# Attention with packed keys and a squared-ReLU MLP on one core: a contiguous first softmax, a new order of the work, and elementwise pieces offered to GpSimd

## The chip, the cores and the metric

The kernel runs on one core of a Trainium2 chip. The metric is the device time of one execution in microseconds. The engines are named as in the profile: PE is TensorE (matmuls; PEld its weight loads), DVE is VectorE, ACT is ScalarE, POOL is GpSimd, SP is SyncE, which here only issues the output DMAs.

## The reference

```python
# q, k, v: (8, 8, 576, 64)   p: (8, 8, 32, 64)   w_in: (512, 2048)   w_out: (2048, 512)
def sm_attn(qq, kk, vv):
    s = scale * np.matmul(qq, kk.transpose(0, 1, 3, 2))     # scale = 1/8
    s = s - np.max(s, axis=-1, keepdims=True)
    a = np.exp(s)
    a = a / (np.sum(a, axis=-1, keepdims=True) + 1e-09)
    return np.matmul(a, vv)
p_packed = sm_attn(p, k, v)                 # first softmax: 32 packed rows over 576 keys
out = sm_attn(q, p_packed, p_packed)        # second softmax: 576 rows over 32 packed keys
x = out.transpose(0, 2, 1, 3).reshape(8 * 576, 512)
r = np.maximum(x @ w_in, 0.0)
return (r * r) @ w_out                      # (4608, 512)
```

## The kernel before

All matmuls are in bf16. The DMAs that POOL issues convert q, k, v, p and the weights from float32 while they load. The work goes batch by batch (eight batches of 576 tokens, eight heads in two halves of four, called qd below), and a batch is cut into named steps:

- Loads: one DMA for each half of k and q, two for v (four in batch 0), eight pieces of w_in, eight of w_out. k and q share twelve buffers, v has four.
- Tk, Tq: DVE transposes a half of k or q in 32x32 blocks (lines 459 and 454). X: p, transposed the same way, is copied into a block-diagonal tile pT_bd (line 407). G: the values are regrouped on DVE (line 430).
- S1: first scores, four matmuls a half (line 467), their maximum (473, 474), the exponential (481), written through a strided view e1x of five groups of 128 columns, in two instructions with two sums, then the sum of these, a reciprocal and the normalising multiplication (489 to 491). E: five transposes on PE (496) and the copy out of PSUM (500).
- PV: packed values (509). XT: copies of their result into the block-diagonal pq_bd (523) and into ppT (516).
- M: the packed values times w_in, so that the second attention's product and the first MLP matmul become one (533, copies 538 and 541).
- S2: second scores, sixteen matmuls (553) and four for the remaining 64 rows (560), which the order puts first from batch 1 on; maximum and subtraction on DVE (572, 577), the exponential on ACT (583), sum, reciprocal and multiplication on DVE (589 to 595; together with the exponential called C). N: ten transposes on PE (602, 605) and copies out (610).
- F1: sixteen blocks of four matmuls for each batch (618), ReLU out of PSUM on ACT (630; in batch 0 in halves on ACT and DVE, 632) into one of four r buffers, and its square on DVE (640; in batch 0 also on ACT, 638) into gT, which holds two batches.
- F2: 36 output tiles of 128 tokens, sixteen matmuls each (648), into one of two PSUM banks, copied out (o_sb, line 653) and stored by four DMAs.

PSUM: two pairs of banks for S1, S2 and F1, two banks for the small steps, two for F2.

The order in which instructions stand in each engine's queue isn't written by hand. A planner (class Plan) knows for every piece an engine or a choice of engines with an assumed cost, the steps it depends on and the buffers it takes; it places the pieces one after the other, the one that can begin earliest first, with a small bias for each stream of steps, and the instructions are then emitted by planned start. On the chip each engine works through its queue in this order and waits on semaphores.

Of the kernel before, what the change touches and what calls it, by code (L numbers as in the profile page):

```python
# [3 lines left out]

# [11 lines left out]
P = 128  # L16
# [5 lines left out]
J0 = (0, 5, 10, 14)  # L22
FB = 128
WCH = 512
BDW = 384
# [5 lines left out]
class Piece:  # L31
    __slots__ = ("step", "stage", "k", "alts", "start", "end", "alt", "pred", "late", "order", "only")

    def __init__(self, step, stage, k, alts):
        self.step, self.stage, self.k, self.alts = step, stage, k, alts
        self.late = self.only = None

class Step:
# [4 lines left out]
    def __init__(self, name, segs, deps=(), take=(), give=(), lag=0.0, banks=(), free=()):  # L44
        self.name, self.deps, self.take, self.give, self.lag = name, list(deps), list(take), list(give), lag
        self.banks = list(banks)
        self.free_at = [[t or name for j, t in free if j == i] for i in range(len(segs))]
        self.pieces = [[Piece(self, i, k, p) for k, p in enumerate(st)] for i, st in enumerate(segs)]
        self.give_at = [[(p, t or name) for p, j, t in self.give if j == i] for i in range(len(segs))]

class Plan:
# [3 lines left out]
    def __init__(self, slots, nbanks):  # L56
        self.nslots, self.nbanks = slots, nbanks
        self.unit = {}
        self.streams, self.base = [], {}
        self.fill = 0  # L60

    def stream(self, prio, steps):
        self.streams.append((prio, list(steps)))

    def forward(self):

        busy = {e: ([-1.0], [t]) for e, t in self.base.items()}
        slots = {k: [] for k in self.nslots}
        last = {k: 0.0 for k in self.nslots}
        held, done, out = {}, {}, []  # L70
        banks = [(0.0, ())] * self.nbanks
        unit = {}
        pos = [0] * len(self.streams)
        since = [0.0] * len(self.streams)
        pend = []

        def ready(st, t):
            pred = []
            for d in st.deps:
                x = done.get(d)  # L80
                if x is None:
                    return INF, pred
                t = max(t, x[0] + HOP)
                pred.append(x)
            for p, n in st.take:
                s = slots[p]
                m = len(s) - self.nslots[p]
                for j in range(max(0, m), m + n):
                    x = s[j]
                    if x is None:  # L90
                        return INF, pred
                    t = max(t, x[0] + HOP)
                    pred.append(x)
                t = max(t, last[p])
            if st.banks:
                u = pick(st, t)
                if u is None:
                    return INF, pred
                for j in u:
                    t = max(t, banks[j][0] + HOP)  # L100
                    pred.append(banks[j])
            return t, pred

        def pick(st, t):
            best = None
            for k, u in enumerate(st.banks):
                if any(banks[j] is None for j in u):
                    continue
                x = max(t, max(banks[j][0] + HOP for j in u)) + 0.001 * k
                if best is None or x < best[0]:  # L110
                    best = (x, u)
            return best and best[1]

        def gap(e, us, t):

            s0, s1 = busy.setdefault(e, ([-1.0], [0.0]))
            i = bisect_right(s0, t) - 1
            t = max(t, s1[i])
            while i + 1 < len(s0) and s0[i + 1] < t + us - 1e-9:
                i += 1  # L120
                t = max(t, s1[i])
            return t, i

        def greedy(pc, t):
            if t == INF:
                return t
            b = None
            for e, us, _ in pc.alts:
                s = t if e == "-" else max(t, busy[e][1][-1] if e in busy else 0.0)
                if b is None or s + us < b[0]:  # L130
                    b = (s + us, s)
            return b[1]

        def book(e, t, f):
            s0, s1 = busy[e]
            i = bisect_right(s0, t) - 1
            if t - s1[i] < 1e-9:
                s1[i] = f
                if i + 1 < len(s0) and s0[i + 1] - f < 1e-9:
                    s1[i] = s1[i + 1]  # L140
                    del s0[i + 1], s1[i + 1]
            elif i + 1 < len(s0) and s0[i + 1] - f < 1e-9:
                s0[i + 1] = t
            else:
                s0.insert(i + 1, t)
                s1.insert(i + 1, f)

        while True:
            best = None
            for i, (prio, steps) in enumerate(self.streams):  # L150
                if pos[i] >= len(steps):
                    continue
                pc = steps[pos[i]].pieces[0][0]
                key = pc.late
                if best is not None and key is not None and key >= best[0]:
                    continue
                t, pred = ready(pc.step, since[i])
                if key is None:
                    key = greedy(pc, t) + 0.02 * prio
                if t < INF and (best is None or key < best[0]):  # L160
                    best = (key, pc, t, pred, i)
            for x in pend:
                key = x[0].late
                if key is None:
                    key = greedy(x[0], x[1]) + 0.02 * (x[2] - 0.5)
                if best is None or key < best[0]:
                    best = (key, x[0], x[1], x[3], x)
            if best is None:
                break
            _, pc, t, pred, src = best  # L170
            src_t = t
            b = None
            for i, (e, us, _) in enumerate(pc.alts):
                if (pc.only is None or pc.only == i):
                    s = t if e == "-" else gap(e, us, t)[0]
                    if b is None or s + us < b[0]:
                        b = (s + us, s, i, e)
            f, s, a, e = b
            pc.start, pc.end, pc.alt, pc.pred = s, f, a, pred
            if e != "-":  # L180
                book(e, s, f)
            out.append(pc)
            st = pc.step
            if pc.stage == 0:
                pos[src] += 1
                since[src] = s
                prio = self.streams[src][0]
                if st.banks:
                    u = unit[st.name] = pick(st, src_t)
                    for j in u:  # L190
                        banks[j] = None
                for p, k in st.take:
                    held[p, st.name] = range(len(slots[p]), len(slots[p]) + k)
                    slots[p] += [None] * k
                    last[p] = s
                ends = [pc]
            else:
                pend.remove(src)
                prio = src[2]
                ends = src[4]  # L200
                ends.append(pc)
                done[f"{st.name}/{pc.stage}.{pc.k}"] = (f, ((pc, 0.0),))
                if len(ends) < len(st.pieces[pc.stage]):
                    continue
            fin = max(p.end for p in ends)
            i = pc.stage
            lag = st.lag
            for p, taker in st.give_at[i]:
                x = (fin + lag, tuple((q, lag) for q in ends))
                for j in held.pop((p, taker)):  # L210
                    slots[p][j] = x
            for taker in st.free_at[i]:
                for j in unit[taker]:
                    banks[j] = (fin + lag, tuple((q, lag) for q in ends))
            if i + 1 < len(st.pieces):
                hop = 0.0 if e == "-" else HOP
                pr = [(fin + hop - HOP, tuple((q, hop - HOP) for q in ends))]
                state = []
                for q in st.pieces[i + 1]:
                    pend.append((q, fin + hop, prio, pr, state))  # L220
            else:
                done[st.name] = (fin + lag, tuple((q, lag) for q in ends))
        assert all(pos[i] == len(s) for i, (_, s) in enumerate(self.streams)) and not pend, [
            s[pos[i]].name for i, (_, s) in enumerate(self.streams) if pos[i] < len(s)]
        self.made = unit
        return out, max(p.end for p in out)

    def backward(self, out, T):
        late = {}
        busy = {}  # L230
# [687 lines left out]
```

## Time and profile before

| what | value |
|---|---|
| median of the runs | 312.61 us (312.1 to 314.21, three runs) |
| profiled execution | 313.22 us, span 311.5 us from the first to the last instruction |
| PE busy | 249.4 us (80%), 1888 matmuls |
| DVE busy | 203.7 us (65%), 437 instructions |
| ACT busy | 183.1 us (59%), 336 instructions |
| POOL busy | 44.4 us (14%), 76 instructions, nearly all issues of DMAs |
| mean granted PE clock | 0.99 |
| loads from HBM, stores | 37.2 MB, 9.4 MB |

Busy is time in which an engine executes; matmuls overlap in PE's pipeline, so a busy PE isn't one at its peak. The share of busy time is a mean over a start in which PE has little to do and a long stretch in which it has nearly always something; a stretch has to be read for itself.

### The profile page before, as it was taken

The numbers are of one execution on the slowest core, as the hardware profiler recorded it, in microseconds if no ns is written. First come the engines' busy times: TensorE is split into PE (matmuls) and PEld (weight loads), VectorE is DVE, ScalarE is ACT, GpSimd is POOL, SyncE is SP. The second block draws the span as 40 slices with busy tenths as digits, with TensorE's granted clock in tenths as the row PEclk, the third lists the DMA queues.
The fourth block names the chain that finished last, engine by engine and source line by source line (L and its number), as shares of the span: only waits on it lengthen the run. The fifth ranks groups of instructions, "written<-read, shape, count | busy, mean of one in ns | idle before, by whom it ended". The sixth has DMA issues, their size and how long they took to land.

```text
span 311.5 us, 5119 instructions
## 1 busy us (share of the span) xinstructions
PE 249.4 (80%) x1888; PEld 139.8 (45%) x1888; DVE 203.7 (65%) x437; ACT 183.1 (59%) x336; POOL 44.4 (14%) x76
## 2 busy tenths in 40 slices
PE   0243596799759888999899889988999799998883
PEld 0141254355526454655455444545454536653331
DVE  6658588879586957777778775786878575540000
ACT  1433287774877566757785767755885577751110
POOL 7655554304000300021000000000000000000000
PEclk9999999999997999999999999999999999999998
DMA  7999999997900691129411102020202111112222
GB/s 120 199 205 206 206 198 207 208 176 137 222 8 0 109 204 43 47 19 209 103 34 36 51 22 58 11 64 3 69 2 67 36 36 34 34 36 64 53 51 67
DMA packets 26456, 28.44 MB, mean 91 GB/s; under 512 B 5440, under 2 KB 17728, under 8 KB 26432
## 3 DMA queue, kind: packets, MB, share of 16 engines
q0 software_dynamic: 18992, 18.55, 37.6%
q1 hardware_dynamic: 6912, 9.45, 11.3%
q8 instruction: 14, 0.23, 0.3%
q10 hardware_dynamic: 528, 0.13, 0.2%
q14 instruction: 10, 0.08, 0.1%
HBM read 37.22 MB, written 9.44 MB: 150 GB/s over the span
## 4 chain that ended last, share of the span: by engine, by line
PE 59%; DVE 20%; ACT 11%; DMA 4%; issue 4%; POOL 1%; SPq 0%; ACTq 0%; DVEq 0%; POOLq 0%
PE ps L648 33%; PE ps L618 14%; ACT o_sb L387 5%; PE ps L553 2%; PE ps L467 2%; DMA v_b<-in_v_dram 2%; PE ps L532 2%; DVE pq_bd L389 2%; PE ps L602 2%; DMA out_dram<-o_sb 2%; DVE t L589 2%; DVE gT L640 2%; ACT pq_bd L387 2%; DVE n L595 1%; PE ps L509 1%
## 5 line engine op out<-in xcount | busy, mean ns | idle before, releaser
L648 PE MATMUL ps<-w_out_b,gT 128*128 128x512 bf16 x576 | 146.8, 380 | 15.9 <-ACT o_sb L387 14.2
L630 ACT ACTIVATE r<-ps 128x576 bf16<-128x576 f32 (+1 forms) x131 | 76.6, 617 | 19.5 <-PE ps L618 16.2
L648 PEld LDWEIGHTS <-gT 128*128 128x128 bf16 x576 | 54.4, 98 | 68.0 <-issue 17.1
L618 PE MATMUL ps<-a,M 128*128 128x288 bf16 x512 | 80.1, 292 | 5.9 <-ACT M L387 2.0
L618 PEld LDWEIGHTS <-M 128*128 128x128 bf16 x512 | 49.5, 99 | 33.6 <-issue 11.2
L640 DVE TENSOR_TENSOR gT<-r 128x576 bf16<-128x576 bf16 x119 | 51.9, 454 | 16.1 <-ACT r L630 15.0
L387 ACT COPY o_sb<-ps 128x512 f32<-128x512 f32 x32 | 18.8, 587 | 33.2 <-PE ps L648 33.2
L387 ACT CAST M<-ps 128x1024 bf16<-128x1024 f32 (+1 forms) x32 | 29.3, 958 | 14.2 <-PE ps L532 13.6
L481 ACT ACTIVATE e1x<-ps,n 128x320 bf16<-128x320 f32 (+1 forms) x32 | 25.3, 904 | 17.9 <-DVE n L474 17.9
L459 DVE STREAM_TRANSPOSE kT<-k_b 128x1152 bf16<-128x1152 bf16 x16 | 21.3, 1358 | 1.1 <-DMA k_b<-in_k_dram 1.1
L454 DVE STREAM_TRANSPOSE qT<-q_b 128x1152 bf16<-128x1152 bf16 x16 | 21.7, 1364 | 0.0
L467 PE MATMUL ps<-kT,pT_bd 128*128 128x288 bf16 x64 | 11.8, 313 | 11.3 <-DVE kT L459 11.1
L419 POOL DMA_DIRECT2D k_b<-in_k_dram x16 | 8.9, 554 | 72.5 <-DVE kT L459 66.1
L387 ACT COPY e<-ps 128x640 bf16<-128x640 bf16 x15 | 10.4, 692 | 12.3 <-PE ps L509 6.3
L389 DVE CAST pq_bd<-ps 32x64 bf16<-32x64 f32 x32 | 7.0, 219 | 14.7 <-ACT r L630 9.8
L532 PE MATMUL ps<-w_in_b,ppT 64*32 64x512 bf16 x256 | 11.5, 409 | 5.6 <-DVE M L389 2.9
L589 DVE TENSOR_REDUCE t<-e 128x36 f32<-128x1152 bf16 (+2 forms) x10 | 11.1, 1110 | 7.2 <-ACT e L583 7.2
L473 DVE TENSOR_REDUCE m<-ps 128x1 f32<-128x576 f32 x16 | 11.9, 742 | 4.6 <-PE ps L467 4.5
L467 PEld LDWEIGHTS <-pT_bd 128*128 128x128 bf16 x64 | 6.7, 104 | 16.5 <-issue 7.4
L572 DVE TENSOR_REDUCE m<-ps 128x4 f32<-128x128 f32 (+2 forms) x17 | 12.2, 719 | 2.1 <-PE ps L553 1.1
L427 POOL DMA_DIRECT2D v_b<-in_v_dram x18 | 12.2, 684 | 5.0 <-DMA k_b<-in_k_dram 1.8
L583 ACT ACTIVATE e<-d 128x1152 bf16<-128x1152 f32 (+2 forms) x10 | 9.7, 972 | 5.0 <-DVE d L577 4.9
(54 smaller groups left out, 197.9 us busy)
## 6 DMA issues: line engine op xcount, KB each, us to landing
out_dram<-o_sb SPq DMA_DIRECT2D x144, 64.0 KB, 1.7
k_b<-in_k_dram POOLq DMA_DIRECT2D x16, 288.0 KB, 8.4
q_b<-in_q_dram POOLq DMA_DIRECT2D x16, 288.0 KB, 10.3
v_b<-in_v_dram POOLq DMA_DIRECT2D x7, 320.0 KB, 10.3
w_in_b<-in_moe_w_in_dram POOLq DMA_DIRECT2D x8, 256.0 KB, 9.4
w_out_b<-in_moe_w_out_dram POOLq DMA_DIRECT2D x8, 256.0 KB, 10.3
v_b<-in_v_dram POOLq DMA_DIRECT2D x7, 256.0 KB, 10.6
v_b<-in_v_dram POOLq DMA_DIRECT2D x2, 160.0 KB, 6.6
```

Source lines behind the costliest of these rows:

```text
L387: nc.scalar.copy(dst, src)
L389: eng.tensor_copy(dst, src)
L454: nc.vector.transpose(self.qT[:, qd].rearrange("p dh (j a) -> p j dh a", a=32), self.t.q[qd][:].rearrange("p (j dh dl) -> p j dh dl", dh=2 ...
L459: nc.vector.transpose(kT[:, qd].rearrange("p dh (j a) -> p j dh a", a=32), self.t.k[qd][:].rearrange("p (j dh dl) -> p j dh dl", dh=2, dl=32))
L467: nc.tensor.matmul(ps[:, c], lhsT=pT_bd[self.b % 2][:, blk(qd, dh)], rhs=kT[:, qd, dh, c * HALF:(c + 1) * HALF], start=(dh == 0), stop=(dh ...
L481: nc.scalar.activation(e[:, i, :, :n], self.ps1[qd][:, :, x0 * 32:(x0 + n) * 32].rearrange("p c (x a) -> p c x a", a=32), ACT.Exp, bias=se ...
L532: nc.tensor.matmul(pair(u, j)[o:o + 32, qd, :], lhsT=self.ppT[64 * e:64 * e + 64, qd, pr, :], rhs=w_in_b[64 * e:64 * e + 64, qd * 2 + pr, ...
L589: nc.vector.tensor_reduce(self.t2[:, g0:g1], self.e2[:, g0:g1], axis=AX.X, op=ALU.add)
L618: nc.tensor.matmul(ps[:, c], lhsT=a.M[:, qd, fb * FB:(fb + 1) * FB], rhs=a.a2[:, qd, c * HALF:(c + 1) * HALF], start=(qd == 0), stop=(qd = ...
L630: nc.scalar.activation(dst, src, ACT.Relu)
L640: eng.tensor_tensor(out=Att.cols(gT[:, fb, o:o + S]), in0=r, in1=r, op=ALU.mult)
L648: nc.tensor.matmul(po[t], lhsT=gT[:, fb, n0:n0 + P], rhs=w_out_b[:, fb, :], start=(fb == 0), stop=(fb == NFB - 1))
```

## The change

Five things change together.

- First softmax. k is loaded in two DMAs per half, so that the keys lie in an order in which the first scores, taken by six matmuls a half (four of 256 columns, two of 64), come out with their 576 columns in the order of the values. The exponential is one contiguous instruction of 576 columns with one sum. The factor 1/8 is put into p when it is expanded, and with it goes the multiplication of the maximum. p is expanded for batches 0 and 1 and for 2 to 7 together, into a tile that holds all batches, instead of batch by batch.
- Smaller copies. ppT is taken in two copies rather than four; M starts from ppT alone, and the sixteen matmuls of the second scores stand ahead of the four.
- Planner. It becomes a list scheduler: at each moment the ready piece with the best priority starts on the engine that ends it first. A table holds a priority for each step and batch and a bias against ACT. The assumed costs are new.
- Choices of engine. Added: ReLU on DVE in batch 1, M's copies on DVE.
- GpSimd (name Q) is offered the squares of F1, the multiplication of the second softmax, the regrouping of the values and the second expansion of p, where POOLED holds the batch (all of them). It also sets zeros (setup2).

The built program of the changed kernel has on POOL 30 squares (in batches 0 to 6: 3, 5, 3, 7, 4, 6 and 2), one multiplication of 128x128 and the memsets; the regrouping and the expansion of p stay on other engines. Its queue of 576 matmuls of F2 is spread otherwise: between the first F1 blocks of successive batches stand 16, 104, 35, 85, 44, 119 and 71 of them (before: 26, 51, 76, 68, 76, 68, 76), 24 within the last batch's blocks (25) and 78 after them (110).

```diff
+TABLE = {'o': {'F1.6': -46.7, 'Tq.4': -34.44, 'E.6': -81.52, 'E.7': 45.46, 'PV.3': -5.85, 'F1.7': -39.65, 'I2':
...
         def setup():
-            nc.vector.memset(pT_bd[0][:, :BDW + 2 * P], 0.0)
-            nc.vector.memset(e1x[:, :, GM * P:], 0.0)
...
+            nc.vector.memset(pT_bd[:, :2], 0.0)
+            nc.vector.memset(v_b[0][:64, :, GM * D:], 0.0)
...
+        def setup2():
+            nc.gpsimd.memset(pT_bd[:, 2:], 0.0)
+            for i in range(1, NV):
+                nc.gpsimd.memset(v_b[i][:64, :, GM * D:], 0.0)
...
+        def expand_p(b0, b1, h, eng):
...
+                eng.tensor_scalar_mul(dst, src, 0.125)
...
+                    src = k[self.b, qd * QH:(qd + 1) * QH].rearrange("h (j2 a x) d -> j2 h a (x d)", j2=2, x=VX)
+                    for j2 in range(2):
+                        nc.gpsimd.dma_start(t[:, j2 * VX * D:(j2 + 1) * VX * D], src[j2])
...
             def s1(self, qd, u):
-                ps = self.ps1[qd] = pair(u)[:, :, :HALF]
-                for c in range(2):
+                ps = self.ps1[qd] = pair(u).rearrange("p c n -> p (c n)")[:, :S]
+                kv = [kT[:, qd, dh].rearrange("p (j2 x a) -> p x j2 a", j2=2, a=32) for dh in range(2)]
+                w = [pT_bd[:, self.b, qd, dh] for dh in range(2)]
+                main = ps[:, :GM * P].rearrange("p (g i n) -> p i g n", i=2, n=64)
+                for i in range(2):
                     for dh in range(2):
-                        nc.tensor.matmul(ps[:, c], lhsT=pT_bd[self.b % 2][:, blk(qd, dh)],
-                                         rhs=kT[:, qd, dh, c * HALF:(c + 1) * HALF], start=(dh == 0), stop=(dh == 1))
+                        nc.tensor.matmul(main[:, i], lhsT=w[dh], rhs=kv[dh][:, i * GM:(i + 1) * GM],
+                                         start=(dh == 0), stop=(dh == 1))
+                for dh in range(2):
+                    nc.tensor.matmul(ps[:, GM * P:], lhsT=w[dh], rhs=kv[dh][:, 2 * GM], start=(dh == 0), stop=(dh == 1))
...
-                e = e1x[:, qd].rearrange("p (g a i2 i) -> p i i2 g a", i=2, i2=2, a=32)
-                for i, n in (0, GM + 1), (1, GM):
-                    x0 = i * (GM + 1)
-                    nc.scalar.activation(e[:, i, :, :n], self.ps1[qd][:, :, x0 * 32:(x0 + n) * 32].rearrange(
-                        "p c (x a) -> p c x a", a=32), ACT.Exp,
-                        bias=self.n1[:, qd:qd + 1], scale=0.125, accum_out=self.d1[:, qd, i:i + 1])
+                nc.scalar.activation(e1x[:, qd], self.ps1[qd], ACT.Exp, bias=self.n1[:, qd:qd + 1],
+                                     accum_out=self.d1[:, qd:qd + 1])
...
+            return [Step(f"G.{b}.0", [[[("DVE", 0.83, lambda: L[b].group(0, H, V))] + ([("POOL", 3.0, lambda: L[b].group(0, H, Q))] if b in POOLED else [])]],
...
-                        [[("DVE", 0.07 + w / 960, lambda: T[b].s2_mul(x, V))]]]
+                        [[("DVE", 0.08 + w / 900, lambda: T[b].s2_mul(x, V))]
+                         + ([("POOL", 0.4 + w / 700, lambda: T[b].s2_mul(x, Q))] if b in POOLED else [])]]
...
-                res = [Step(nr, [r] + front(2, 128), pre, banks=AB, free=[(2, None)]),
-                       Step(nm, [a] + front(3, 1024), pre, banks=HB, free=[(2, None)]),
+                res = [Step(nm, [a] + front(3, 1024), pre, banks=HB, free=[(2, None)]),
+                       Step(nr, [r] + front(2, 128), pre, banks=AB, free=[(2, None)]),
...
+                sq = [("DVE", 0.46, lambda fb=fb: f1_sq(T[b], fb, V))]
+                if b in SPLIT:
+                    sq.append(("ACT", 0.68, lambda fb=fb: f1_sq(T[b], fb, A)))
+                if b in POOLED:
+                    sq.append(("POOL", 0.95, lambda fb=fb: f1_sq(T[b], fb, Q)))
...
+        POOLED = range(B)
...
+                                          + ([("POOL", 1.0, lambda h=h: expand_p(2, B, h, Q))] if POOLED else []) for h in range(QH)]], ["P.2", "I2"])])
...
+        ld += load_wo(range(0, 4)) + [Step("I2", [[[("POOL", 5.0, setup2)]]])]
...
+        plan.use(TABLE)
+        est = plan.run()
```

## The prediction

> **What bounds the kernel now.** I read the page's table of slices first (where PE is thin), then busy time in ten stretches cut at the first F1 matmul (L618) of each of the eight batches, then the waits of PE, then groups by form. Columns of the first view: from:to, length, busy time and (instructions) of each engine, granted PE clock, DMA share, GB/s.
>
> ```profile
> 0.00:37.60 37.60, 11.23 (x101) 6.79 (x102) 23.79 (x59) 12.14 (x24) 22.60 (x40) 1.00 1.14 187
> 37.60:66.80 29.20, 23.31 (x190) 12.91 (x190) 24.43 (x48) 21.94 (x49) 11.12 (x19) 1.00 1.27 204
> 66.80:99.10 32.30, 27.00 (x218) 15.81 (x217) 25.00 (x54) 22.13 (x40) 3.54 (x6) 0.95 0.54 103
> 99.10:132.90 33.80, 30.54 (x242) 17.35 (x240) 24.52 (x53) 22.34 (x41) 3.55 (x6) 1.00 0.50 93
> 132.90:164.20 31.30, 28.87 (x233) 16.45 (x232) 24.07 (x52) 22.25 (x39) 3.54 (x6) 1.00 0.50 91
> ...
> 276.90:311.50 34.60, 25.34 (x115) 10.98 (x113) 0.90 (x2) 4.75 (x8) 0.00 (x0) 0.96 0.24 61
> ```
>
> Up to 66.8 us PE is not the bound: the loads run at 187 to 204 GB/s and DVE is busy 24 of 37.6 and 24 of 29.2 us. From 99 us on PE is (30.5 of 33.8 us). The next view is who PE waited for after 66.8 us: total us, times, longest.
>
> ```profile
> PE ps L648 <- ACT o_sb L387: 14.2, 23, 0.7
> PE ps L560 <- DVE ppT L389: 6.2, 6, 1.6
> PE ps L618 <- ACT M L387: 2.0, 1, 2.0
> PE ps L618 <- ACT e1x L481: 0.8, 1, 0.8
> PE ps L648 <- DVE gT L640: 0.5, 1, 0.5
> PE ps L532 <- DVE d L577: 0.4, 1, 0.4
> ```
>
> A second output tile starts only after the copy of the one before it, 0.6 us each time (14.2/23): the largest item. Then the four matmuls of the rest of the second scores (L560), which stand ahead of the main sixteen (L553), wait about 1 us in six batches for the ppT copies. The rest falls into the third stretch, and there the clock shows it too:
>
> ```profile
> 84.00:90.00 6.00, 3.87 (x54) 1.95 (x52) 4.95 (x14) 3.92 (x8) 0.00 (x0) 1.00 0.24 79
> 90.00:96.00 6.00, 3.59 (x34) 2.10 (x26) 4.39 (x6) 4.67 (x6) 0.00 (x0) 0.82 0.01 3
> 96.00:99.00 3.00, 3.00 (x21) 1.92 (x21) 1.36 (x4) 1.99 (x4) 0.00 (x0) 0.79 0.00 0
> ```
>
> PE stood idle 4.5 of 12 us between 84 and 96, and the granted clock of 0.82 and 0.79 follows. Prices for the engines that the change moves work between:
>
> ```profile
> L640 DVE TENSOR_TENSOR gT<-r 128x576 bf16<-128x576 bf16 x119 | 51.9, 454 | 16.1 <-ACT r L630 15.0
> L481 ACT ACTIVATE e1x<-ps,n 128x320 bf16<-128x320 f32 x16 | 15.7, 979 | 17.9 <-DVE n L474 17.9
> L481 ACT ACTIVATE e1x<-ps,n 128x256 bf16<-128x256 f32 x16 | 13.3, 829 | 0.0
> L481 ACT ACTIVATION_READ_ACCUMULATOR e1x<-ps,n 128x1 f32 x32 | 8.7, 271 | 0.0
> L425 POOL MEMSET v_b<- 128x512 bf16 x3 | 1.6, 543 | 0.0
> masks.py:199 POOL TENSOR_SCALAR_AFFINE_SELECT ident<-ident 128x128 bf16<-128x128 bf16 x1 | 0.3, 287 | 0.1
> ```
>
> **The work on PE.** Back to back, 12 matmuls of L648 take 2.76 us in the timeline and 16 take 3.61: 0.213 each, 576 of them 122.9 us. A block of four F1 matmuls takes 0.49 (8 take 1.14, 4 take 0.65): 128 blocks, 62.7 us. Everything else of a batch (first scores 1.0, transposes and values 1.1, second scores 1.15, M 1.1, second transposes 0.6) is 4.95 us, 39.6 in all. Sum 225.2; the other 86.3 us of the 311.5 are lost, 43.5 of them before 66.8 us.
>
> **First softmax made contiguous.** Per half batch ACT drops 979 + 829 + 2 x 271 = 2.35 us for one exponential over 576 columns and one accumulator read. The nearest row is the ReLU over 128x576 from PSUM, 652 ns; the second softmax's exp, 1,165 ns for 1,152, gives 0.6. I take 0.68 + 0.27 = 0.95, so 1.4 us less, 22 us of ACT over 16 halves. DVE loses two small operations (154 and 138 ns) and 64 columns of 390 ns per half, about 5 us in all; the 32 expanding copies of 204 ns (6.5 us) become some 3 us. All of this is ACT and DVE time, 22 of 31 us per steady batch, so after 99 us it is worth nothing by itself; its cover is PE's own queue. It does shorten the way from first scores to second transposes. On PE six matmuls take the place of four with the same columns: about 0.08 us per half (two more fills), **+1.3 us**.
>
> **The start.** The setup on DVE is priced like before. Transposing the second k tile ahead of the values removes 2.1 us at 10.8 us, and the attention of batch 0 is then 2 to 4 us early. But the next steps need loads, and these hold no fewer bytes: waits of the queue for its eighth-last transfer put the landing of k of batch 1 at 31.7 and 33.1, of v at 36, of q at 40 and 41.4, of the late p at 45.5. In the new order DVE stands in line at each of them: its transposes of batch 1 come at 31.8, 33.6, 39.9 and 41.8 us and the transpose of p, with the ReLU half of F1 block 2 and the pq copies queued behind it, only at 45.5. I get the first F1 matmul at 37.4 (37.6 before) and, with 17.3 us of DVE work after p and a tenth of waiting, F1 of batch 1 at 65 instead of 66.8. By then PE has 1.8 us less behind it (16 matmuls of L648 against 26): **0**. GpSimd's new memsets (3,072 columns at 543/512 = 1.06 ns, and three of 543 ns: 4.9 us) stand ahead of k of batch 1, its split into two DMAs costs 0.55 us more issue per tile, and what hides both is the 8 to 10 us between issue and landing; without that cover they cost up to 4.9 us.
>
> **The second scores.** In the new order the sixteen matmuls stand ahead of the four, and they need the pq copies alone, with 2 to 4 us of other PE work since the values matmuls. The six waits at L560 after 66.8 us go: **-6.2** (between -6.2 and 0; the lower waits of the sixteen show 1.7 us in one batch, so I keep it whole).
>
> **The third stretch.** The new order puts attention of batches 2 and 3 and 104 matmuls of L648 into the stretch that held one batch and 51; by the prices 39.6 us of PE against 37 of DVE. So the waits there on M, e1x, gT and d (3.7 us) and the slow clock (F1 blocks of eight at 1.45 to 1.83 instead of 1.14, about 1.5 us) have 11 us more of matmuls beside them: 5.2 to 0, I take **-3.1**, since nine F1 blocks in a row there run at ACT's 0.65 and not at PE's 0.49, and DVE is nearly full.
>
> **GpSimd.** In the built program it takes 30 squares and one small multiplication (128x128); the regrouping of values stays on DVE, the expansion of p on DVE and ACT. DVE loses 30 x 0.454 = 13.6 us, which is off the path. A square on GpSimd is bounded by 576 x 1.06 = 0.61 us and 576 x 287/128 = 1.29 us; I take 1.3, since the second row reads what it writes, as a square does. For 28 of the 30 PE has 5.7 to 27 us of other work between the F1 block and the first matmul that reads it; two have 2.4 and 3.8 us, and ReLU plus square take about 2.1. In the one run of five (batch 3, blocks 0 to 4) the four r buffers are just enough: 5 x (1.3 - 0.8) = 2.5 us against three spacings of 0.8. **+1.0** (0 to 3). Loads queued behind squares are needed 50 us later or more.
>
> A rule speaks against this part. The Trainium skill (SBUF — State Buffer, "Who interferes with whom") says that a VectorE instruction with two SBUF inputs and a GpSimd instruction that reads SBUF exclude each other for the whole instruction. No instruction of this kind ran on GpSimd here, so no row shows it; taken fully, each of the 30 squares could hold up DVE by its own length, 39 us on an engine with 100 us free.
>
> **The sum.** Output tiles still follow each other directly 21 times (19 to 20 before), so the 14.2 us stay. -6.2 - 3.1 + 1.3 + 1.0 + about 0.5 for the run of F1 blocks = -6.5. The profiled execution took 313.2 us around its span of 311.5; that gives 306.7, and as the median of the runs lies 0.6 under the profiled one, **306.1 us**.
>
> **The rivals.** (1) More is won: all of the third stretch, and the steady waits of the PE queue thin out because a square now has at least 1.8 us of PE work before its reader (20 squares had less than 2.0 before, one has now). -6.2 - 5.2 + 1.8 and another 3 to 4 us: about 299. For it: DVE and ACT together lose some 50 us. Against it: PE's listed waits after 66.8 us, tiles aside, are only 10 us. (2) Nothing is won: the memsets let the load queue run dry, everything up to batch 2 is 4 us late, and half of the third stretch stays: 311. Against it stand the 8 to 10 us of lead. A tie is also what comes if the waits at L560 reappear at the sixteen matmuls. (3) Slower, by one mechanism: GpSimd's squares are longer, by themselves or by waiting for DVE, and the four r buffers stop F1. With x us per square the run of five costs 5(x - 0.8) - 2.4 and three runs of three 3(x - 0.8) - 2.4 each. At x = 2.0 that is 3.6 + 3 x 1.2 = 7.2 and eats the gain, at 2.6 it is 15.6 and the kernel takes about 321. It decides from 2 us per square.
>
> **How the numbers follow.** Forecast (302 to 309) 0.47, rival 1 0.19, rival 2 0.17, rival 3 0.17. Faster by over 1% (what a measurement of this kernel can tell from no change) is the forecast and rival 1, 0.66. The range takes rival 1's 299 with half a per cent under it, and reaches up through rival 2 to the beginning of rival 3: 297.5 to 316.
>
> **What would show it.** The waits of PE after: L503 (the former L560) under 2 us in all, o_sb still 13 to 15 us; F1 of batch 1 begins at 63 to 67 us; the stretch with two batches shows a clock of 1.00; GpSimd squares under 1.5 us each and DVE squares still near 0.45. I am wrong if ReLUs wait for GpSimd's gT, if DVE squares grow well over 0.5 us, or if new waits of PE stand where L560's were.

## The result and the profile after

The changed kernel takes 322.66 us (median of four runs, 321.13 to 323.52) beside 312.89 us of the kernel before (312.1 to 314.21, four runs): a ratio of 1.030, 95% interval 1.027 to 1.033. The forecast was 306.1 us, 297.5 to 316. It is slower, at the price of the third rival, though not by its mechanism.

The stretches of the changed kernel, cut at the first F1 matmul (L561) of batches 0 to 3, and the last batch (columns as in the prediction):

```profile
0.00:41.10 41.10, 12.52 (x109) 8.48 (x109) 24.59 (x48) 10.73 (x23) 29.71 (x46) 1.00 1.10 169
41.10:82.40 41.30, 25.35 (x181) 13.38 (x181) 21.14 (x45) 20.43 (x40) 18.13 (x26) 0.76 1.08 158
82.40:129.70 47.30, 43.86 (x367) 23.93 (x365) 35.76 (x58) 28.34 (x53) 16.31 (x21) 0.99 0.67 108
...
282.00:321.70 39.70, 30.95 (x167) 16.06 (x165) 8.71 (x18) 12.71 (x21) 0.00 (x0) 0.97 0.19 49
```

The first two stretches took 82.4 us where the prediction has 65: +17.4. From there to the end of the span it is 239.3, where the prediction's span of 305.0 (311.5 less 6.5) leaves 240.0. So the whole error lies ahead of F1 of batch 1. Who PE waited for up to 82 us (us in total, times, longest):

```profile
PE ps L410 <- DVE kT L399: 17.4, 3, 11.4
PE ps L591 <- POOL gT L583: 9.6, 1, 9.6
PE ps L434 <- DVE e1n L428: 3.7, 2, 2.0
```

One wait of 9.6 us for a square on POOL stands out. The timeline of POOL tells what it did before it (start, length, what, idle time before it and what ended that):

```profile
23.48 2.68 POOL L331 MEMSET pT_bd<- 128x3072 bf16 x1
26.07 1.48 POOL L333 MEMSET v_b<- 64x512 bf16 x3
27.48 2.77 POOL L362 DMA_DIRECT2D k_b<-in_k_dram  x4
...
66.06 0.69 POOL L367 DMA_DIRECT2D v_b<-in_v_dram  x1 [1.68 <-DMA v_b<-in_v_dram]
67.15 0.57 POOL L358 DMA_DIRECT2D q_b<-in_q_dram  x1 [0.40 <-issue]
68.56 0.54 POOL L358 DMA_DIRECT2D q_b<-in_q_dram  x1 [0.85 <-DMA q_b<-in_q_dram]
69.12 3.36 POOL L583 TENSOR_TENSOR gT<-r 128x576 bf16<-128x576 bf16 x3
```

Each load here waits until an earlier one has landed: in the kernel before, every issue from the ninth on to the end of batch 4's loads starts 0.28 to 0.55 us after the landing of the eighth-last one. The loads of batches 2 to 4 keep POOL until 69.1 us. Then it does the three squares of batch 0, blocks 7 to 9, 1.15 us each. The planner counts an issue at 0.55 to 1.1 us and knows no such wait: by the times that it works out POOL is through with these loads at 42.7 us and begins the squares at 45.4. The squares themselves are no longer than forecast (count, then busy us and mean ns):

```profile
L583 POOL TENSOR_TENSOR gT<-r 128x576 bf16<-128x576 bf16 x30 | 35.2, 1188 | 133.4 <-ACT r L573 133.4
L583 DVE TENSOR_TENSOR gT<-r 128x576 bf16<-128x576 bf16 x90 | 43.8, 496 | 29.8 <-ACT r L573 28.7
```

And the loads come in more slowly from the first microsecond on (the GB/s of the 40 slices, then the packets; first the kernel before, then the changed one):

```profile
GB/s 120 199 205 206 206 198 207 208 176 137 222 8 0 109 204 43 47 19 209 103 34 36 51 22 58 11 64 3 69 2 67 36 36 34 34 36 64 53 51 67
DMA packets 26456, 28.44 MB, mean 91 GB/s; under 512 B 5440, under 2 KB 17728, under 8 KB 26432
```

```profile
GB/s 49 190 204 201 195 193 194 190 187 70 0 25 169 142 194 88 92 35 25 59 199 60 45 35 34 33 26 44 39 40 71 50 35 33 50 49 28 46 60 65
DMA packets 41016, 28.50 MB, mean 89 GB/s; under 512 B 17952, under 2 KB 34336, under 8 KB 40992
```

The first slice moves 49 GB/s where the kernel before has 120, with 17,952 packets under 512 bytes against 5,440; of those in the queue of the loads 13,584 have 4 bytes (1,072 before). The first scores begin at 11.4 us, not 8.5.

So the theory for the experiments was: A, the split k loads start everything some 3 us later; B, the memsets ahead of k of batch 1 cost about as much; C, three squares behind loads in POOL's queue cost 9.6 us and a slow clock. Rival 1 was the prediction's own third: GpSimd's squares are long or hold up DVE, all thirty. Rival 2: the loads bound the start whatever is done.

### The profile page after: what moved, and what is told of

It is laid out like the page before. It is cut to its first block, busy times and chain, and to the rows that moved or that the text cites. A ratio compares the mean times of both kernels' runs of the same rounds, so it can differ in the third digit from the quotient of the medians.

```text
span 321.7 us, 5114 instructions
## 1 busy us (share of the span) xinstructions
PE 254.9 (79%) x1920; PEld 143.7 (45%) x1920; DVE 195.5 (61%) x344; ACT 165.7 (52%) x293; POOL 95.5 (30%) x122
## 2 busy tenths in 40 slices
DMA packets 41016, 28.50 MB, mean 89 GB/s; under 512 B 17952, under 2 KB 34336, under 8 KB 40992
## 4 chain that ended last, share of the span: by engine, by line
PE 62%; DMA 18%; ACT 7%; DVE 4%; POOL 3%; issue 3%; ACTq 0%; DVEq 0%; POOLq 0%
PE ps L591 36%; PE ps L561 16%; DMA q_b<-in_q_dram 6%; DMA k_b<-in_k_dram 4%; ACT o_sb L319 4%; DMA p_b<-in_p_dram 4%; DMA w_in_b<-in_moe_w_in_dram 3%; ACT r L573 2%; DVE o_sb L321 2%; PE ps L475 2%; PE ps L496 2%; PE ps L410 1%; DMA out_dram<-o_sb 1%; PE ps L545 1%; PE ps L434 1%
## 5 line engine op out<-in xcount | busy, mean ns | idle before, releaser
L591 PE MATMUL ps<-w_out_b,gT 128*128 128x512 bf16 x576 | 150.8, 380 | 24.6 <-ACT o_sb L319 9.9
L573 ACT ACTIVATE r<-ps 128x576 bf16<-128x576 f32 (+1 forms) x134 | 79.6, 612 | 42.3 <-PE ps L561 36.5
L561 PE MATMUL ps<-a,M 128*128 128x288 bf16 x512 | 86.6, 297 | 4.9 <-DVE r L575 2.0
L591 PEld LDWEIGHTS <-gT 128*128 128x128 bf16 x576 | 53.9, 98 | 69.2 <-issue 15.1
L583 POOL TENSOR_TENSOR gT<-r 128x576 bf16<-128x576 bf16 x30 | 35.2, 1188 | 133.4 <-ACT r L573 133.4
L561 PEld LDWEIGHTS <-M 128*128 128x128 bf16 x512 | 50.4, 101 | 40.6 <-issue 15.3
L583 DVE TENSOR_TENSOR gT<-r 128x576 bf16<-128x576 bf16 x90 | 43.8, 496 | 29.8 <-ACT r L573 28.7
L319 ACT CAST M<-ps 128x1024 bf16<-128x1024 f32 (+1 forms) x30 | 27.2, 944 | 21.1 <-PE ps L475 16.5
L319 ACT COPY o_sb<-ps 128x512 f32<-128x512 f32 x24 | 14.1, 586 | 31.3 <-PE ps L591 30.7
L362 POOL DMA_DIRECT2D k_b<-in_k_dram x32 | 22.7, 714 | 12.5 <-DVE kT L399 6.8
L410 PE MATMUL ps<-kT,pT_bd 128*128 128x256 bf16 x64 | 11.3, 306 | 17.5 <-DVE kT L399 17.4
L321 DVE COPY o_sb<-ps 128x512 f32<-128x512 f32 x12 | 8.2, 690 | 27.3 <-PE ps L591 27.1
L421 ACT ACTIVATE e1x<-ps,n 128x576 bf16<-128x576 f32 x16 | 11.9, 743 | 14.3 <-DVE n L417 14.2
L417 DVE TENSOR_REDUCE n<-ps 128x1 f32<-128x576 f32 x16 | 11.9, 746 | 5.5 <-PE ps L413 5.5
L358 POOL DMA_DIRECT2D q_b<-in_q_dram x16 | 8.9, 564 | 16.4 <-DVE qT L394 11.4
```

The costliest lines, as they stand in the source:

```text
L319: nc.scalar.copy(dst, src)
L321: eng.tensor_copy(dst, src)
L362: nc.gpsimd.dma_start(t[:, j2 * VX * D:(j2 + 1) * VX * D], src[j2])
L410: nc.tensor.matmul(main[:, i], lhsT=w[dh], rhs=kv[dh][:, i * GM:(i + 1) * GM], start=(dh == 0), stop=(dh == 1))
L417: nc.vector.tensor_reduce(self.n1[:, qd:qd + 1], self.ps1[qd], axis=AX.X, op=ALU.max, negate=True)
L561: nc.tensor.matmul(ps[:, c], lhsT=a.M[:, qd, fb * FB:(fb + 1) * FB], rhs=a.a2[:, qd, c * HALF:(c + 1) * HALF], start=(qd == 0), stop=(qd = ...
```

## The experiments

**Three squares on DVE.** In the changed kernel:

```diff
         def f1_sq(a, fb, eng):
+            if eng is Q and a.b == 0:
+                eng = V
```

> Three of the 30 squares, those of blocks 7 to 9 of batch 0, run on DVE at the same place of the order; everything else is as in the changed kernel. Theory: they stood on POOL behind loads whose issue had to wait, PE waited 9.6 us for them in one go, and the granted clock fell behind that pause: about 11 us less, 308 to 313 us, F1 of batch 1 near 71 us and no slow clock between 64 and 88 us. Rival 1 (a GpSimd square is too long or holds up DVE, each of the 30 alike): a tenth of the loss goes, 320 us or more. Rival 2 (the start is bound by the loads themselves, and the next step waits for the same loads): less than 3 us.

Measured: 310.71 us, ratio to before 0.992 (0.990 to 0.995); 12.0 us less than the changed kernel, by three of thirty squares. Rival 1 is out as the main cause. F1 of batch 1 begins at 69.5 us, and the three squares now run at 58.3, 60.4 and 61.3 us instead of from 69.1 on. Two more views, first of the changed kernel, then of this one, for the same six microseconds each, show the rest of the loss (columns as above; the clock is third from the end):

```profile
66.00:72.00 6.00, 1.66 (x11) 0.43 (x19) 0.00 (x0) 0.00 (x0) 4.68 (x6) 0.50 1.38 184
72.00:78.00 6.00, 4.94 (x44) 1.78 (x29) 2.20 (x5) 3.37 (x5) 0.48 (x1) 0.50 0.60 107
```

```profile
66.00:72.00 6.00, 4.67 (x34) 2.91 (x35) 4.68 (x11) 4.40 (x7) 1.40 (x3) 1.00 1.37 176
72.00:78.00 6.00, 5.51 (x37) 3.38 (x35) 5.94 (x9) 5.08 (x8) 2.75 (x3) 1.00 0.71 125
```

Behind the wait of 9.6 us the granted clock is 0.50; with the wait gone it stays at 1.00. Between the first F1 of batch 0 and that of batch 1 lie 28.7 us instead of 41.3: 12.6, of which 9.6 are the wait; the other 3 fall into the stretch with the slow clock.

**The memsets earlier, alone.** `setup2()` is called right behind the identity, ahead of the weights:

> The memsets on POOL are issued right behind the loads of k, v and q of batch 0, before the first load of weights, instead of right ahead of k of batch 1; the rest is as in the changed kernel. Theory: k of batch 1 lands some 3 us earlier, POOL reaches its three squares some 3 us earlier, and the time falls by 2 to 4 us to 319 to 321. Rival (the memsets were hidden, as the prediction had it, or the weights are now late): 322 to 324.

Measured: 321.17 us, 1.026 (1.021 to 1.030), 1.5 us under the changed kernel, and the runs of the two overlap (319.71 to 323.15, 321.13 to 323.52). F1 of batch 1 begins 2.8 us earlier in the profiled execution, at 79.6, as the theory says, but the time is too close to settle anything.

**One DMA for each half of k, order made by the matmul.**

```diff
-                kv = [kT[:, qd, dh].rearrange("p (j2 x a) -> p x j2 a", j2=2, a=32) for dh in range(2)]
+                kv = [kT[:, qd, dh].rearrange("p (j2 x a) -> p x a j2", j2=2, a=32) for dh in range(2)]
```

> Each half of k is loaded by one DMA again, with 18 keys in a row on each partition as before; the first scores read their columns of kT with a stride of 288 instead, so that they still come out in the order of the values. The rest is as in the changed kernel. Theory: the 12,000 packets of 4 bytes go, the first k lands near 7 us instead of 10, all loads of the start are 3 us earlier: 318 to 321 us. Rival 1 (only the first step is earlier, the loads behind it are bound by bytes): 322 to 323. Rival 2 (the matmuls pay for the strided read): twice the time of 96 matmuls with 18,432 columns, about 7 us more, 326 to 330.

Measured: 321.64 us, 1.026 (1.021 to 1.031), in none of the three ranges. The effects of the theory and of rival 2 are both there and nearly cancel: F1 of batch 1 begins at 73.4 instead of 82.4, but the first scores pay in every batch. The matmuls that read kT, first in the run with three squares on DVE, then here (min/median/max ns):

```profile
L410 PE MATMUL ps<-kT,pT_bd x64: 269/273/421, 11.1 to 222.3; 128*128 128x256 bf16 x64
```

```profile
L406 PE MATMUL ps<-kT,pT_bd x64: 402/405/422, 7.1 to 233.2; 128*128 128x256 bf16 x64
```

The six of a half take 1.26 us instead of 0.66, 7.2 us over the twelve halves of batches 2 to 7.

**All three edits.**

> All three edits together: three squares on DVE, the memsets early, one DMA for each half of k. Theory: the three losses lie one behind the other on the way to F1 of batch 1, which begins at 64 to 67 us as forecast; 304 to 308 us, less than before's 312.9. Rival 1 (long squares): above 316. Rival 2 (the same loads): 309 to 313, no more than the first edit gives.

Measured: 313.84 us, 1.004 (1.001 to 1.006). The time misses the 304 to 308 of the theory. F1 of batch 1 begins at 65.8, as it says, but the strided reads cost more than this gains: it is 3.1 us slower than with the three squares alone (310.71). The order of keys has to be made somewhere else.

**Order made by the loads of the values.** k is loaded as before the change; the values go to partitions 64 i + 32 j2 + a instead:

```diff
-                src = v[self.b].rearrange("h (ap x) d -> ap h (x d)", x=VX)
-                nc.gpsimd.dma_start(self.v_raw[64 * i:64 * i + 64, :, :n * D], src[:, :, i * GM * D:(i * GM + n) * D])
+                src = v[self.b].rearrange("h (a j2 x) d -> j2 a h (x d)", j2=2, x=VX)
+                for j2 in range(2):
+                    o = 64 * i + 32 * j2
+                    nc.gpsimd.dma_start(self.v_raw[o:o + 32, :, :n * D], src[j2, :, :, i * GM * D:(i * GM + n) * D])
```

With three squares on DVE, and the memsets early or at the changed kernel's place:

> Three squares on DVE and the memsets early, as in the run with all three edits, but the order of the keys is made another way: each half of k is loaded by one DMA, and the values are loaded in that order instead, by four DMAs of 32 partitions a batch in place of two of 64, so that the first scores read kT without the stride of 288. Theory: F1 of batch 1 begins near 66 us and the 7 us of the strided reads are gone: 304 to 308 us. Rival (the load order only moves the 4 byte packets to the values, or six DMAs a batch hold up the start as much): 309 to 312.

> As the run before it, but with the memsets where the changed kernel has them, ahead of k of batch 1. Theory: the memsets cost 1 to 3 us more than in the run before it, 306 to 310 us. Rival (they are hidden): the same within half a microsecond.

Measured: early 308.46 us, 0.986 (0.983 to 0.989); late 306.17 us, 0.978 (0.976 to 0.981). The late place is better, against both the theory and its rival, so B falls: at their place the memsets are hidden, as the prediction had it, and moving them up costs 2.3 us. (Behind the early memsets the first load of w_in is issued at 10.4 instead of 6.4 us, k of batch 1 lands at 32.0 instead of 30.3, and the first F1 begins at 39.9 instead of 38.0. By F1 of batch 1 little of that is left, 66.0 against 65.7, and the two profiled executions differ by 0.35 us only, so how the medians come to 2.3 is open.) From 310.71 to 306.17 the split of k is worth 4.5 us.

**No squares on POOL.**

> As the run with three squares on DVE, early memsets and values in the order of k, but all 30 squares run on DVE at the same places of the order. Theory: the other 27 squares on POOL cost and bring nothing: within 1.5 us of that run. Rival 1 (GpSimd's squares are long or hold up DVE): faster by 3 us or more. Rival 2 (DVE needs the relief): slower by 3 us or more.

Measured: 308.29 us, 0.984 (0.982 to 0.987), beside 308.46: the other 27 squares neither cost nor bring anything that can be measured.

**The split of k in the kernel before, and the squares alone in the changed one.**

> The kernel before, with nothing changed but that each half of k is loaded by two DMAs with the changed kernel's pattern; the keys are then in another order than the values, so the sums of the first attention are over other pairs, and the time is read alone. Theory: the first k lands 3 us later, and as the start is bound by loads up to 60 us, 2 to 4 us are lost: 315 to 317 us. Rival (the first step alone is later and is caught up with behind it): 312.5 to 314.

> The changed kernel with the values in the order of k (one DMA for each half of k) and nothing else: the memsets and the three squares of batch 0 stay on POOL at their places. Theory: the loads are some 4 us earlier, but the three squares still stand behind the loads of batches 2 to 4 and cost about 8 us at one wait: 313 to 316 us, F1 of batch 1 near 73 us. Rival (with the loads earlier POOL reaches the squares in time): 306 to 309.

Measured: 316.83 us, 1.011 (1.008 to 1.014), so A alone costs 3.7 us in the kernel before, with F1 of batch 1 at 70.2 instead of 66.8. And 316.62 us, 1.011 (1.007 to 1.015): with A gone C is still there, one wait of 8.6 us, 10.5 us more than with the squares on DVE. That is a little more than the 313 to 316 expected, and F1 of batch 1 begins at 76.4, not near 73. Of the 16.5 us between the changed kernel and 306.2 the squares are worth 12.0 when they are moved first and 10.5 when the loads are put right first, the split 6.0 or 4.5: the two overlap by 1.5 us.

**Is it the engine or its queue?** All thirty squares on POOL, but loads held back until they are through: first those of batches 2 to 4 behind block 9 of batch 0, then also those of batches 3 and later behind the five squares of batch 1.

```diff
+            if a.b == 0 and fb == 9:
+                opened.append(1)
+                for f in held:
+                    f()
```

> As the run before it, all 30 squares on POOL, but the loads of k, v and q of batches 2 to 4 that stood ahead of the three squares of batch 0 are issued behind the third of them. Theory: it is the place in POOL's queue, not the engine, that cost: 306 to 309 us, as with the three squares on DVE. Rival 1 (the square on GpSimd is too slow for this place): 312 or more. Rival 2 (the later loads are now late for batch 2): F1 of batch 1 near 66 us, but the stretch behind it is longer by 3 us or more.

> All 30 squares on POOL and values in the order of k; the loads of k, v and q of batch 2 are issued behind the third square of batch 0, those of batches 3 and later behind the fifth square of batch 1, so that no square of these two batches stands behind a load that must wait. Theory: with the place in the queue put right, GpSimd costs nothing: 306 to 309 us, as with the three squares on DVE (306.2). Rival 1 (GpSimd itself is too slow for these squares): F1 of batch 2 later than 118 us, 311 or more. Rival 2 (the loads of batch 3 are now late): first scores of batch 3 wait for k, 309 to 314.

Measured: 315.86 us, 1.010 (1.006 to 1.013), and 316.93, 1.013 (1.011 to 1.015). Neither reaches the 306 to 309 of its theory, but both show where it goes. In the first, F1 of batch 1 begins at 64.5 us, 1.2 earlier than with the squares on DVE: GpSimd is fast enough for this place. Rival 2 comes nearest: the stretch behind it takes 57.2 us, 9.5 more than with the squares on DVE. The held loads now stand ahead of batch 1's squares, and a ReLU waits for an r buffer (its timeline, with POOL's):

```profile
79.74 0.55 POOL L358 DMA_DIRECT2D q_b<-in_q_dram  x1 [0.83 <-DMA q_b<-in_q_dram]
80.30 2.26 POOL L581 TENSOR_TENSOR gT<-r 128x576 bf16<-128x576 bf16 x2
81.49 0.65 ACT L571 ACTIVATE r<-ps 128x576 bf16<-128x576 f32 x1 [5.25 <-POOL gT L581]
```

PE waits those 5.25 us too, and its granted clock is 0.68 from 78 to 84 us. Not all of this is the queue: while POOL works off its three late squares, a square on DVE takes 3.53 us (from 82.2) instead of about 0.45.

In the second no engine waits for a square on POOL between 60 and 125 us, and now the values of batch 3 are late (POOL, then DVE):

```profile
85.24 1.15 POOL L581 TENSOR_TENSOR gT<-r 128x576 bf16<-128x576 bf16 x1 [7.32 <-ACT r L571]
86.33 1.12 POOL L358 DMA_DIRECT2D k_b<-in_k_dram  x2
...
95.90 0.83 DVE L321 COPY v_g<-v_b 128x2560 bf16<-128x2560 bf16 x1 [6.23 <-DMA v_b<-in_v_dram]
```

POOL sat idle 7.3 us for its fifth square while the loads behind it were due, and PE then waits 5.2 us for the first scores of batch 3. F1 of batch 2 begins at 123.3: the numbers are those of rival 1, but the five squares of batch 1 take 1.14 to 1.20 us, and the mechanism is that of rival 2. In neither of the two orders does the one queue hold both: whichever stands first, the other is late. Other orders weren't tried.

**What is slow in the split loads?** Kernel before, k cut by columns (two DMAs of [128][576], same rows of 2,304 bytes read) or by heads (four of [32][2][576]):

> The kernel before with each half of k loaded by two DMAs, but cut by columns: each takes 576 of the 1,152 elements of every partition, and the keys stay as they were. Theory: the packets of 4 bytes come with rows whose heads can't be merged into one stride, so this has about 1,100 of them as before, and the first scores begin at 8.5 to 9.5 us. Rival: they come with the rows of 576 elements, so it has some 13,000, and the first scores begin at 11 us.

> The kernel before with each half of k loaded by four DMAs, one for a head, each with both runs of 576 elements for 32 partitions, which gives the changed kernel's order of keys (the time is read alone, since the sums are then over other pairs). Theory, as for the cut by columns: no packets of 4 bytes beyond some 1,100, since a head alone has one stride for its partitions; eight issues of about 0.55 us in place of two. Rival: rows of 576 elements bring them, some 13,000.

Measured, one run each: 313.85 and 315.73 us, with 1,328 and 1,840 packets of 4 bytes; the first scores begin at 7.4 and 7.9 us, against 11.2 with the changed kernel's split of the same rows and 8.5 in the kernel before. The small packets can be counted out: in these two and in the kernel before there are 16 for each load (83, 115 and 67 loads); the split has 384 more for each of its 32 DMAs of k. The packet lines of that split in the kernel before and of the cut by columns:

```profile
DMA packets 41048, 28.49 MB, mean 90 GB/s; under 512 B 17984, under 2 KB 34368, under 8 KB 41024
```

```profile
DMA packets 28760, 28.44 MB, mean 91 GB/s; under 512 B 5696, under 2 KB 22080, under 8 KB 28736
```

So what goes with the slow transfer is neither the row length nor the second DMA, but a source whose outermost dimension is the four heads. Between 3 and 4 us of the span, when only k is on its way, the loads move 6 KB with the changed kernel's split and 115 KB with the cut by columns. The Trainium skill (DMA: Bandwidth & Descriptors, "Why a DMA increments its semaphore by 16 and not by 1") states that the number of DMA engines a transfer uses is the largest up to 16 that divides the slowest dimension of both sides. By that rule, as an estimate, 4 heads would give four engines, 128 or 32 partitions sixteen. The runs agree: in that microsecond 3.6 data packets are in flight on average with the split in the kernel before and 3.0 in the changed kernel, but 15.5 with the cut by columns, 15.7 with that by heads and 15.5 in the kernel before. The records don't name the engine of a packet, and what the additional small packets are for isn't shown.

The cut by heads still takes 315.73 us beside 312.69 of the kernel before, 3.0 us more, where the slow split cost 3.7; with one run, and eight issues a batch in place of two, what the pattern alone costs isn't separated from the number of issues.

**The output banks.** The prediction carried 14.2 us of waits for the copies o_sb as fixed. They aren't waits for a bank: the plan gives successive tiles the two banks nearly always in turn, but both are halves of one tile, and the second matmul of a new output tile is emitted behind the copy of the old one.

```diff
-        ps = [psum.tile([P, 2, 512], F32, name=f"ps{i}") for i in range(4)]
+        ps = [psum.tile([P, 2, 512], F32, name=f"ps{i}") for i in range(3)]
+        po_bank = [psum.tile([P, 512], F32, name=f"po{i}") for i in range(2)]
...
-            t = ps[u[j] // 2][:, u[j] % 2, :]
+            t = po_bank[u[j] - 6][:] if u[j] > 5 else ps[u[j] // 2][:, u[j] % 2, :]
```

> As the fastest version so far (three squares on DVE, values in the order of k, late memsets; 306.2 us), but the two PSUM banks of the output tiles are two tiles instead of halves of one. The waits of PE for the copies o_sb, 14.6 us in 24 places in that run, were carried as fixed in the prediction. Theory: a new output tile goes to the other bank, and PE waits only since both banks belong to one tile; the waits go and the time falls by 11 to 15 us to 291 to 295. Rival 1 (the bank itself is still busy): no change. Rival 2 (PE is then held by DVE, ACT or a lower clock): 297 to 303.

> The kernel before with the same edit alone: two tiles for the two banks of the output. Theory: its o_sb waits, 14.2 us after 66.8 us, go as well: 298 to 302 us. Rival (no false wait): 312 to 314.

> The version with two tiles for the two output banks (287.4 us), with all 30 squares on DVE at the same places. Theory: DVE has room everywhere behind the start, and the 27 squares bring nothing: within 1.5 us of 287.4. Rival 1 (now that PE no longer pauses, DVE is nearer to the bound and GpSimd's help counts): 289 to 293. Rival 2 (GpSimd's squares hold up): 282 to 285.5.

Measured: 287.43 us, 0.918 (0.916 to 0.921), the fastest version; the kernel before with this edit 294.91, 0.943 (0.939 to 0.946); and without squares on POOL 287.78, 0.920 (0.919 to 0.922), so GpSimd is worth nothing here either. PE at the end of the run, in the version before this edit and then with it:

```profile
288.14 3.61 PE L591 MATMUL ps<-w_out_b,gT 128*128 128x512 bf16 x16 [0.78 <-DVE o_sb L321]
292.47 3.61 PE L591 MATMUL ps<-w_out_b,gT 128*128 128x512 bf16 x15 [0.72 <-ACT o_sb L319]
```

```profile
263.73 16.57 PE L592 MATMUL po<-w_out_b,gT 128*128 128x512 bf16 x75
```

No wait for o_sb is left in the list of PE. Sixteen matmuls come 4.33 us apart with the wait and 3.5 without. The gain is larger than expected, 18.7 us where the listed waits were 14.6, and in the kernel before 17.8 where they were 14.2. An estimate from the timeline closes most of that: back to back the matmuls of L591 start 0.215 us apart and are listed with 0.38 each, so that each overlaps the next by 0.16, and a stop loses this overlap too. 24 stops lose 3.9 us, which makes 18.5.

## Why the prediction was wrong

- **The start, priced at 0, is the step that failed.** It cost 17.4 us in the profiled runs and 16.5 in the medians, in two terms. First: "Loads queued behind squares are needed 50 us later or more" looked at the loads behind the squares in POOL's queue, not at the squares behind the loads. The prediction used the same rule of the queue, a load waits for its eighth-last, to date the landings; applied to what stands behind the loads, it gives the wait: in the kernel before the last load of batch 4 is issued at 59.9 us, and the squares stand behind it, while on DVE they run at 58.3 to 61.3 us even with the slow loads. Measured 10.5 to 12.0 us; in the changed kernel 9.6 of it are one wait. Second: the split of k was priced by its issue, 0.55 us per tile, on the assumption that transfers of the same bytes take the same time. Measured 3.7 us in the kernel before and 4.5 to 6.0 here.
- **The memsets** were right: 4.2 us on POOL (4.9 forecast), hidden by the loads in flight: ahead of k of batch 1 they hold its issue up by 3.5 us, and its first piece still lands 1.4 us after the load before it (34.1 after 32.7).
- **GpSimd's squares** were right in size (1.15 to 1.19 us, 1.3 taken). The price of the feared rule, the port that VectorE and GpSimd share (the Trainium skill, SBUF — State Buffer, "Who interferes with whom"), would by the prediction's estimate have been up to 39 us; the run without any square on POOL takes 308.29 us against 308.46. Squares on DVE beside those on POOL do get longer, as the last section shows, but by some 4 us in all.
- **The rest of the sum holds as a total, and that is in part luck.** With the two terms taken away the kernel takes 306.17 us, forecast 306.1; F1 of batch 1 begins at 65.7 (65), and 239.7 remain to the end of the span (240.0). Three terms missed, in both directions. The two more fills of the six matmuls (+1.3) are a cost that no run shows: six take 0.66 us a half where four took 0.65. The +1.0 for squares on POOL is within the noise. And of the 6.2 us at the second scores 1.5 are left, as a wait for a copy of M; the waits for ppT are gone. The o_sb waits stay at 14.4 us (14.6 with the two terms taken away). The exponential of 576 columns is 0.74 us (0.68). What the third stretch alone brought (-3.1) wasn't measured by itself.
- **The rivals.** The third gave about the right time, 321, for a wrong reason: its point, a mean of 2 us per square, was not reached (1.19; one of thirty took 2.08), and no ReLU of the changed kernel is listed as waiting for a square on POOL. What it lacked was the same engine's queue. The o_sb term was right as a size and wrong as a fact of the kernel: it was the largest thing to be won.

## What to carry to other kernels

Before elementwise work is put on the engine that issues the loads, date each piece by its place in that queue, with the waits of the loads ahead of it; its idle share (86% here) says nothing of that. A load that is cut differently is priced by its pattern, not by its bytes: compare the first slices of GB/s and the small packets. And a recurring wait on "the other buffer" is worth a look at what unit the dependency is kept for: two halves of one tile are one buffer.

## What the runs showed of the hardware

- In a pause of PE of 9.6 us (60.7 to 70.3 us) the granted clock fell to 0.74 between 60 and 66 us; it stood at 0.50 from 66 to 78 us and was still 0.55 from 78 to 84, with PE at work again.
- A source pattern of four heads times 32 partitions goes with some 13,600 packets of 4 bytes, 49 to 53 GB/s in the first slice and 3.0 to 3.6 data packets in flight (the changed kernel; the kernel before with that split); the same rows as 128 partitions at one stride with 1,328, 123 and 15.5.
- Matmuls of 256 columns whose moving operand goes to and fro between two places 288 elements apart take 405 ns, against 273 with runs of 32.
- VectorE and GpSimd do hold each other up at times. Squares on DVE take 496 ns on average in the changed kernel and 450 with none on POOL, which is some 4 us over 90 of them; eight take more than 600 ns, each beside a square on POOL. In one place a square on POOL took 2.08 us instead of 1.15 while DVE was in a multiplication with two inputs, and of the two DVE squares behind that one was held to 1.40 (1.77 for both; POOL first, then DVE):

```profile
136.84 2.08 POOL L583 TENSOR_TENSOR gT<-r 128x576 bf16<-128x576 bf16 x1 [0.53 <-ACT r L573]
```

```profile
136.57 1.34 DVE L538 TENSOR_TENSOR n<-e,r 128x1152 bf16<-128x1152 bf16 x1
137.83 1.77 DVE L583 TENSOR_TENSOR gT<-r 128x576 bf16<-128x576 bf16 x2
```
